# Decode attention with an MLP on one Trainium2 core: which queue issues wq, x, b2 and the first K tiles, and what the second K tile waits for

## The chip, the cores and the metric

The kernel runs on 1 core of one Trainium2 chip. The metric is the device time of one execution in microseconds. Beside the times there is one profiled execution. Its span is counted from the first to the last instruction of the program, and all positions in time below are counted from the start of that span.

## The reference

One decode step for 8 sequences (B = 8, one query each): layernorm, attention over a cache of 4096 keys with 32 heads of 128, an MLP on the same normalized input, and a residual. All inputs are bf16.

```python
def _A_ref(x, k_cache, v_cache, wq, wo):          # caches: 8 x 32 x 4096 x 128
    q = (x @ wq) as 8 x 32 x 1 x 128
    scores = jnp.einsum("bhqd,bhkd->bhqk", q, k) * (Dh ** -0.5)
    p = _softmax(scores, axis=-1)
    o = jnp.einsum("bhqk,bhkd->bhqd", p, v)
    return o as 8 x 1 x 4096 @ wo

def _B_ref(x, w1, b1, w2, b2):                     # w1: 640 x 1728, w2: 1728 x 640
    y = _layernorm(x, axis=-1)
    h = _gelu(jnp.einsum("bsd,df->bsf", y, w1) + b1)
    return jnp.einsum("bsf,fd->bsd", h, w2) + b2

xn = _layernorm(x, axis=-1)                        # x: 8 x 1 x 640
return x + _A_ref(xn, ...) + _B_ref(xn, ...)
```

Each cache has 268 MB, wq and wo 5.24 MB each, w1 and w2 2.2 MB each. Every byte of them is needed once.

## The kernel before

The work is cut into 32 tiles (`NQ`), one for each pair of a sequence and a group of 8 heads. A tile needs 8.39 MB of K and 8.39 MB of V, each as 128 partitions of 64 KB. SBUF holds three slots of that size: `KA` and `KB` for K tiles of even and odd number, and `VS` for V. In what follows K0, K1, V0 and so on are the tiles by number.

The slots hold other things before their first tile. `wq_sb` lies in `VS` (line 269), so V0 may only be loaded once the q matmuls have read it. `b2_sb`, `x_sb`, the two normalized inputs, the masks' scratch and a block of zeros lie in `KB` (lines 280 to 290), so K1 may only be loaded once these have been read. K0 goes to `KA`, which is free from the start.

For a tile, VectorE multiplies 176 of the 256 key positions of each partition with q, adds halves and sums (`dve_chunk`, three chunks), while TensorE, ScalarE and TensorE again transpose, copy and multiply the other 80 (`pe_T`, `act_T`, `pe_QK`). `dve_max` forms the maximum, `act_exp` the exponentials with their sums, `pe_PV` multiplies with V in 256 matmuls, `act_O` and `o_norm` finish the tile's output.

The program is written as steps with a position each (`at(pos, step)`, lines 791 to 882). The steps are sorted by position, and each engine's list of instructions is what the steps give it in that order. An engine runs its list in order and stops at a wait. VectorE, ScalarE and TensorE have their tiles' part as a hardware loop; SyncE and GpSimd have theirs written out. A wait that an engine has already made for the same or a later count of the same semaphore is left out (`_Eng.wait`, line 51).

SyncE's list before: wq (position -890), K0 (-870), a wait for the q matmuls (`tk["qmm"]`, set in `pe_q`), K1 (position 49), V0 (50; its own wait for `qmm` is left out, being made already), then for each further tile K(i) (position 100i - 51) and V(i) (100i + 50). `load_k` for i from 2 on waits for the last transposes and the last VectorE chunk of tile i - 2 (`kt`, `km`); `load_v` for i from 1 on waits for the PV matmuls of tile i - 1 (`pv`). The order is K0, K1, V0, K2, V1, K3, V2 and so on, each behind the one before it in the one queue. Behind the caches follow w1, w2 and wo: w1 and w2 wait for tile 30's K slot, wo for tile 31's.

ScalarE's list before begins with the loads of x (-900) and b2 (-898). Then it loads a table and takes the square roots for the two layernorms (`norm`).

TensorE's list at the start: `pe_xT(0)` transposes the normalized x, `pe_xT(1)` the twice normalized one for the MLP, `pe_acc0` sets the accumulator `ACC_ps` to x + b2 by 11 matmuls that read zeros, `x_sb` and `b2_sb`, and `pe_q` computes q by 160 matmuls once wq has landed. `cp_q` (VectorE) copies q to SBUF, `qrep` (GpSimd) spreads tile 0's part of it, `pe_qbc` and `act_qbc` bring that to all partitions, and `dve_chunk(0, 0)` needs both this and K0.

In the tail, `pe_mlp1` computes the hidden layer into `HT_ps` (14 blocks of 8 columns; the last is the remainder of 1728 after 13 blocks of 128), `act_gelu` applies gelu in one instruction for 13 blocks and one for the last, and `pe_mlp2` adds its product with w2 to `ACC_ps`. The rows of wo are added in `fin_wl` and `fin_wn`, and `fin_store` writes the result.

Of the kernel before, what the change touches and what calls it, by code (L numbers as in the profile page):

```python
# [11 lines left out]
ACT = mybir.ActivationFunctionType  # L12
AX = mybir.AxisListType

P = 128
# [177 lines left out]
def bass_parallel_sum__gqa_block_cached__mixer_channel_mlp__decode_kernel(  # L193
# [13 lines left out]
    B, _, D = A_x.shape  # L207
# [8 lines left out]
    DC = D // P  # L216
    FB = F // P
# [23 lines left out]
    def kslot(i):  # L241
        return KA if i % 2 == 0 else KB
# [5 lines left out]
    x2 = A_x.rearrange("b s d -> (b s) d")  # L248
    out2 = out.rearrange("b s (c n) -> (b s c) n", n=P)

    with ExitStack() as es:
# [7 lines left out]
        def part(slot, lo, n, rows=P):  # L259
            return S_sb[0:rows, slot, lo:lo + n]  # L260
# [3 lines left out]
        def scratch(n, rows=P, slot=KB):  # L264
            ap = part(slot, o_[slot], n, rows)
            o_[slot] += n + n % 2
            return ap

        wq_sb = part(VS, 0, DC * H * DH).rearrange("p (c n) -> p c n", c=DC)
        w1_sb = scratch(DC * F, P, KA).rearrange("p (c n) -> p c n", c=DC)  # L270
        w2_sb = scratch(FB * D, P, KA).rearrange("p (c n) -> p c n", n=D)
        hT_sb = scratch((FB + 1) * B, P, KA).rearrange("p (c b) -> p c b", b=B)
# [7 lines left out]
        b2_sb = scratch(D, 1)  # L280
        x_sb = scratch(D, B)
# [11 lines left out]
        ones_sb = sb("ones_sb", [1, B], BF)  # L293
# [35 lines left out]
        ACC_ps = ps("ACC_ps", [P, 512], F32)  # L329
# [3 lines left out]
        HT_ps = TR_ps[:, 1, :].bitcast(F32)[:, 0:(FB + 1) * B]  # L333
# [4 lines left out]
        pe, dve, act, sp, pool = (_Eng(sem(f"{n}_s")) for n in ("pe", "dve", "act", "sp", "pool"))  # L338
        pe2, act2 = _Eng(sem("pe2_s")), _Eng(sem("act2_s"))
        ld_s = [_Dma(sem(f"ld_s{s}")) for s in range(3)]  # L340
        ld_x, ld_b1, ld_b2, ld_wq, ld_w1, ld_w2a, ld_w2b, st_o = (
            _Dma(sem(n)) for n in ("ld_x", "ld_b1", "ld_b2", "ld_wq", "ld_w1", "ld_w2a", "ld_w2b", "st_o"))
# [3 lines left out]
        tk = {}  # L346
        prog = []

        def at(pos, fn, *a):
            prog.append((pos, len(prog), fn, a))  # L350
# [4 lines left out]
        def cache_src(cache, i):  # L355
            hq, b = divmod(i, B)
            return cache[b, hq * HS:(hq + 1) * HS].rearrange("h (p j) d -> (h p) j d", j=NKEY)

        def load_k(i):
            s = kslot(i)  # L360
            if i >= 2:
                sp.wait(tk[("kt", i - 2)], tk[("km", i - 2)])
            elif s == KB:
                sp.wait(tk["qmm"])
            tk[("k", i)] = ld_s[s].sig(sp.dma_start(tile[s], cache_src(A_k_cache, i)))

        def load_mlp():
# [123 lines left out]
        def pe_acc0():  # L491
            pe.wait(tk["consts"], tk["x"], tk["b2"], tk["id"])
            pe.matmul(ACC_ps[:, 0:DC * B], zeros_sb, zeros_sb[:, 0:DC * B], start=True, stop=False,
                      skip_group_check=True)
            for c in range(DC):
                pe.matmul(ACC_ps[:, c * B:(c + 1) * B], x_sb[:, c * P:(c + 1) * P], ident_bf[0:B, 0:B],
                          start=False, stop=False, skip_group_check=True)
                pe.matmul(ACC_ps[:, c * B:(c + 1) * B], b2_sb[:, c * P:(c + 1) * P], ones_sb[:, :],
                          start=False, stop=False, skip_group_check=True)

        def widen():
            pool.wait(tk["w1"], tk["b1"])
# [19 lines left out]

        def act_gelu():
            TRB[1].use(act)
            act.activation(hT_sb[:, 0:FB, :].rearrange("p c b -> p (c b)"), HT_ps[:, 0:FB * B],
                           ACT.Gelu_apprx_tanh)
            tk["h"] = TRB[1].used(act, act.sig(act.activation(
                hT_sb[:, FB, :], HT_ps[:, FB * B:(FB + 1) * B], ACT.Gelu_apprx_tanh)))

# [259 lines left out]


        Q = 100.0
        at(-900, load, "x", ld_x, x_sb, x2, act)
        at(-898, load, "b2", ld_b2, b2_sb, B_b2.rearrange("(o f) -> o f", o=1), act)
        at(-890, load, "wq", ld_wq, wq_sb, A_wq.rearrange("(p c) n -> p c n", c=DC))
        at(NQ * Q - 55, load_mlp)
        at(-870, load_k, 0)
        at(-798, zero_w2b)
        at(-800, consts_pool)
# [7 lines left out]
        at(-773, pe_xT, 1)  # L806
        at(-772, cp_xT, 1)
        at(-771, pe_acc0)
        at(-770, pe_q)
        at(-765, cp_q)  # L810
        at(NQ * Q - 11.8, load_b1)
        at(NQ * Q - 11.7, widen)
        at(NQ * Q - 11.5, pe_mlp1)
        at(NQ * Q - 11, act_gelu)
        at(NQ * Q + 4.6, pe_mlp2, range(FB))
        for i in range(NQ):
            o = i * Q
            last = i == NQ - 1
            if i:
                at(o - 51, load_k, i)  # L820
            at(o + 50, load_v, i)
            at(o - 52, qrep, i)
            at(o - 2, k_ready, i)
            at(o - 11, pe_qbc, i)
            at(o - 10.5, act_qbc, i)
            nt = jp_of(i) // TPB
            w = 42.0 / nt
            for t in range(nt):
                at(o + w * t, pe_T, i, t)
                at(o + w * (t + 0.4), act_T, i, t)  # L830
                at(o + w * (t + 1.5), pe_QK, i, t)
            at(o + 2, dve_chunk, i, 0)
            at(o + 26, dve_chunk, i, 1)
            at(o + 52, dve_sel, i, 0)
            at(o + 55, dve_sel, i, 1)
            at(o + 58, dve_chunk, i, 2)
            at(o + 84, dve_max, i)
            at(o + 90 if i else o + Q + 45, act_exp, i)
            at(o + Q + 48, pe_RS, i)
            at(o + Q + 57, dve_rinv, i)  # L840
            at(o + Q + 50, pe_PV, i)
            if not last:
                at(o + Q + 71, act_O, i)
            at(o + Q + 75, o_norm, i)
# [3 lines left out]
        o = NQ * Q  # L848
# [78 lines left out]
```

## Time and profile before

| | us |
|---|---|
| median of 3 runs (lowest, highest) | 1282.06 (1282.04, 1282.07) |
| the profiled execution's own time | 1281.86 |
| its span | 1280.5 |
| VectorE busy | 1104.0 |
| TensorE busy | 672.4 |
| ScalarE busy | 476.3 |
| GpSimd busy | 105.0 |

Nearly every row of the profile names line 111, because a helper replays all recorded instructions from there; the groups are told apart by the tiles that they write and read. `S_sb` is the tensor with the three slots, `KT_sb` and `TR_ps` belong to the transposes, `S_ps` to the scores of TensorE's share, `PV_ps` to the product with V, `CH_ps` to q, `ACC_ps` to the final sums. `SPq` and `ACTq` rows are DMA issues by SyncE and ScalarE. In a row of the timeline the first number is the start, the second the length, both in us, then the engine, the instruction, output and inputs and their shapes; in brackets stands how long the engine had been idle and what ended it. One row can merge several instructions (x2, x160), and then its length runs from the start of the first to the end of the last. The trace also holds a record of each packet that a DMA engine moved, with its start, length, bytes and queue; q1 is SyncE's queue, q10 ScalarE's.

### The profile page before, as it was taken

The page shows a single profiled execution, that of the slowest core. Times are in us where ns is not written, and L with a number is a line of the kernel's source. Part 1 is how long each engine was busy: PE and PEld are TensorE (multiplying, and loading weights), DVE is VectorE, ACT ScalarE, POOL GpSimd, SP SyncE. Part 2 cuts the span into 40 slices and gives each one's busy share as a digit, 9 for nine tenths or more (in the row PEclk, how much of TensorE's full clock was granted, in tenths as well). Part 3 has the DMA queues.
Part 4 walks back from the last instruction along what each step waited for, and adds up shares of the span by engine and source line. Part 5 has one row for each costly group of instructions (what it writes and reads, how often), then busy time and mean ns, then how long its engine had stood idle before and what let it go on. Part 6 is the DMA issues. An engine that isn't in the chain of part 4 may idle for free.

```text
span 1280.5 us, 34441 instructions
## 1 busy us (share of the span) xinstructions
PE 672.4 (53%) x13944; PEld 576.2 (45%) x13944; DVE 1104.0 (86%) x680; ACT 476.3 (37%) x905; POOL 105.0 (8%) x113
## 2 busy tenths in 40 slices
PE   1546555446645446545456555456454466454476
PEld 1435444335535345434345444345344355353365
DVE  1899999889888889888899888898888898888895
ACT  0524444233444233443234443234443234442331
POOL 0020000000000000000000000000000000000040
PEclk9755555555555555555556555555655565555555
DMA  9999999999999999999999999999999999999998
GB/s 423 423 435 428 434 432 434 436 432 432 430 442 432 432 430 442 428 434 432 440 428 432 434 434 436 430 434 430 442 430 430 432 442 430 432 430 444 423 436 364
DMA packets 10675, 551.99 MB, mean 431 GB/s; under 512 B 1244, under 2 KB 1445, under 8 KB 1702
## 3 DMA queue, kind: packets, MB, share of 16 engines
q1 hardware_dynamic: 10592, 551.79, 99.7%
q8 instruction: 9, 0.15, 0.0%
q10 hardware_dynamic: 70, 0.03, 0.0%
q14 instruction: 4, 0.03, 0.0%
HBM read 551.80 MB, written 0.01 MB: 431 GB/s over the span
## 4 chain that ended last, share of the span: by engine, by line
DMA 52%; DVE 36%; issue 11%; DVEq 0%; PE 0%; SPq 0%; ACT 0%
DMA S_sb<-in_A_k_cache_dram 51%; DVE S_sb L111 26%; DVE Sd_sb L111 8%; DMA S_sb<-in_A_wo_dram 2%; DVE S_ps L111 1%; DVE ri_sb L111 0%; DVEq L109 0%; PE ACC_ps L111 0%; DVE mx_sb L111 0%; SPq L111 0%; DVE mbT_sb L111 0%; DVE mxT_sb L111 0%; DVE mq_sb L111 0%; DVE mb_sb L111 0%; PE QB_ps L111 0%
## 5 line engine op out<-in xcount | busy, mean ns | idle before, releaser
L111 PE MATMUL TR_ps<-ident_bf,S_sb 128*128 128x128 bf16 (+1 forms) x2570 | 343.3, 285 | 354.0 <-POOL kr_sb L111 342.7
L111 DVE TENSOR_TENSOR S_sb<-S_sb,qbc_sb 128x7552 bf16<-128x7552 bf16 (+1 forms) x96 | 392.5, 4088 | 128.5 <-DMA S_sb<-in_A_k_cache_dram 128.1
L111 PEld LDWEIGHTS TR_ps<-ident_bf,S_sb 128*128 (+2 forms) x2570 | 245.7, 104 | 411.3 <-issue 338.6
L111 DVE TENSOR_REDUCE Sd_sb<-S_sb 128x59 f32<-128x3776 bf16 (+1 forms) x96 | 390.2, 4065 | 6.0
L111 ACT ACTIVATE KT_sb<-TR_ps 128x1024 bf16<-128x1024 bf16 x320 | 326.7, 1023 | 122.3 <-PE TR_ps L111 110.4
L111 PE MATMUL PV_ps<-P_sb,S_sb 128*128 128x8 bf16 x8192 | 224.0, 175 | 135.6 <-DMA S_sb<-in_A_v_cache_dram 133.1
L111 PEld LDWEIGHTS PV_ps<-P_sb,S_sb 128*128 128x128 bf16 x8192 | 221.4, 103 | 138.3 <-DMA S_sb<-in_A_v_cache_dram 135.7
L111 DVE TENSOR_TENSOR S_sb<-S_sb 128x3776 bf16<-128x3776 bf16 (+1 forms) x96 | 205.4, 2139 | 3.3
L111 ACT ACTIVATE P_sb<-Sd_sb,NB_sb 128x256 bf16<-128x256 f32 x256 | 126.3, 494 | 214.6 <-DVE NB_sb L111 214.6
L111 PE MATMUL S_ps<-qrep_sb,KT_sb 128*128 128x8 bf16 x2560 | 122.3, 177 | 52.1 <-ACT KT_sb L111 49.0
L111 ACT ACTIVATE oU_sb<-PV_ps 128x8 f32<-128x8 f32 x31 | 5.5, 177 | 375.0 <-PE PV_ps L111 375.0
L111 PEld LDWEIGHTS S_ps<-qrep_sb,KT_sb 128*128 128x128 bf16 x2560 | 92.4, 104 | 83.7 <-ACT KT_sb L111 40.5
L111 POOL TENSOR_TENSOR oT_sb<-oU_sb,ri_sb 128x8 bf16<-128x8 f32 x31 | 71.7, 2312 | 374.8 <-DVE S_sb L111 315.3
L111 POOL COPY qrep_sb<-qT_sb 128x128 bf16<-128x128 bf16 x32 | 18.1, 566 | 474.2 <-PE S_ps L111 455.5
L111 ACT ACTIVATION_READ_ACCUMULATOR P_sb<-Sd_sb,NB_sb 128x1 f32 x256 | 47.8, 187 | 0.0
L111 DVE TENSOR_TENSOR S_ps<-S_ps,mask_sb 128x320 f32<-128x320 f32 (+1 forms) x65 | 31.6, 486 | 2.6 <-PE S_ps L111 2.6
L111 DVE TENSOR_REDUCE Sd_sb<-S_ps 128x40 f32<-128x320 f32 x64 | 31.5, 492 | 2.2
L111 PE MATMUL QB_ps<-ident_bf,qrep_sb 128*128 128x128 bf16 x32 | 9.1, 284 | 40.6 <-DVE S_sb L111 21.4
L111 ACT ACTIVATE qbc_sb<-QB_ps 128x128 bf16<-128x128 f32 x32 | 8.9, 277 | 57.1 <-PE QB_ps L111 57.1
L111 POOL MEMSET kr_sb<- 128x1 f32 x32 | 3.1, 98 | 295.0 <-DMA S_sb<-in_A_k_cache_dram 295.0
L111 PEld LDWEIGHTS QB_ps<-ident_bf,qrep_sb 128*128 128x128 bf16 x32 | 3.3, 103 | 43.4 <-ACT oU_sb L111 26.5
L111 PE MATMUL CH_ps<-rs_sb,ones_f 128*128 128x8 f32 x64 | 16.8, 337 | 6.4 <-ACT P_sb L111 6.4
(73 smaller groups left out, 149.0 us busy)
## 6 DMA issues: line engine op xcount, KB each, us to landing
S_sb<-in_A_v_cache_dram SPq DMA_DIRECT2D x1, 6144.0 KB, 26.8
S_sb<-in_A_wq_dram SPq DMA_DIRECT2D x1, 5120.0 KB, 15.3
S_sb<-in_A_wo_dram SPq DMA_DIRECT2D x1, 2560.0 KB, 15.8
S_sb<-in_B_w_dram SPq DMA_DIRECT2D x1, 2160.0 KB, 30.3
S_sb<-in_B_w_dram SPq DMA_DIRECT2D x1, 2080.0 KB, 34.8
S_sb<-in_A_v_cache_dram SPq DMA_DIRECT2D x1, 2048.0 KB, 31.3
S_sb<-in_A_wo_dram SPq DMA_DIRECT2D x1, 1280.0 KB, 18.5
S_sb<-in_A_wo_dram SPq DMA_DIRECT2D x1, 800.0 KB, 20.0
```

What stands on the lines that cost most here:

```text
L111: inst = getattr(e, name)(*a, **k)
```

## The change

The first loads change queues: x and b2 go from ScalarE's list to SyncE's, wq from SyncE's to ScalarE's. The positions stay, so that SyncE's list begins with x, b2, K0 and ScalarE's with wq.

`pe_acc0` gets a signal on its last matmul (`tk["acc0"]`), and K1 waits for that instead of the q matmuls. V0's own wait for the q matmuls now stands in SyncE's list, between K1 and V0.

`act_gelu` takes the 13 blocks in two instructions (6 and 7 blocks), so that gelu has three.

```diff
@@ load_k
             elif s == KB:
-                sp.wait(tk["qmm"])
+                sp.wait(tk["acc0"])
             tk[("k", i)] = ld_s[s].sig(sp.dma_start(tile[s], cache_src(A_k_cache, i)))
@@ pe_acc0
             for c in range(DC):
                 pe.matmul(ACC_ps[:, c * B:(c + 1) * B], x_sb[:, c * P:(c + 1) * P], ident_bf[0:B, 0:B],
                           start=False, stop=False, skip_group_check=True)
-                pe.matmul(ACC_ps[:, c * B:(c + 1) * B], b2_sb[:, c * P:(c + 1) * P], ones_sb[:, :],
-                          start=False, stop=False, skip_group_check=True)
+                last = pe.matmul(ACC_ps[:, c * B:(c + 1) * B], b2_sb[:, c * P:(c + 1) * P], ones_sb[:, :],
+                                 start=False, stop=False, skip_group_check=True)
+            tk["acc0"] = pe.sig(last)
@@ act_gelu
-            act.activation(hT_sb[:, 0:FB, :].rearrange("p c b -> p (c b)"), HT_ps[:, 0:FB * B],
-                           ACT.Gelu_apprx_tanh)
+            for lo, hi in ((0, FB // 2), (FB // 2, FB)):
+                act.activation(hT_sb[:, lo:hi, :].rearrange("p c b -> p (c b)"), HT_ps[:, lo * B:hi * B],
+                               ACT.Gelu_apprx_tanh)
@@ the steps
-        at(-900, load, "x", ld_x, x_sb, x2, act)
-        at(-898, load, "b2", ld_b2, b2_sb, B_b2.rearrange("(o f) -> o f", o=1), act)
-        at(-890, load, "wq", ld_wq, wq_sb, A_wq.rearrange("(p c) n -> p c n", c=DC))
+        at(-900, load, "x", ld_x, x_sb, x2)
+        at(-898, load, "b2", ld_b2, b2_sb, B_b2.rearrange("(o f) -> o f", o=1))
+        at(-890, load, "wq", ld_wq, wq_sb, A_wq.rearrange("(p c) n -> p c n", c=DC), act)
```

## The prediction

> **What bounds the kernel now.** I read the page's head first, for the span and the share of the DMA engines, then its list of queues, then the timeline of the first 140 us, and last the timeline of the tail.
>
> ```profile
> span 1280.5 us, 34441 instructions
> ...
> PE 672.4 (53%) x13944; PEld 576.2 (45%) x13944; DVE 1104.0 (86%) x680; ACT 476.3 (37%) x905; POOL 105.0 (8%) x113
> ...
> DMA  9999999999999999999999999999999999999998
> ...
> q1 hardware_dynamic: 10592, 551.79, 99.7%
> ...
> HBM read 551.80 MB, written 0.01 MB: 431 GB/s over the span
> ```
>
> VectorE is busy for 86% of the span, but the 16 DMA engines are busy in every slice, and SyncE's queue alone fills 99.7% of them. The windows view gives 433 GB/s for each of 300:600, 600:900 and 8:1270. So the time is a start of about 2 us, 552 MB at 433 GB/s, and a short tail. A change of issue order can move that only if it starts the stream earlier or later, lets the queue run empty, or lengthens the tail.
>
> ```profile
> 0.74 0.38 SPq L111 DMA_DIRECT2D S_sb<-in_A_wq_dram  x1
> 0.75 0.59 ACTq L111 DMA_DIRECT2D S_sb<-in_A_x_dram  x1
> ...
> 1.18 19.71 SPq L111 DMA_DIRECT2D S_sb<-in_A_k_cache_dram  x2
> ...
> 16.10 4.43 PE L111 MATMUL CH_ps<-xT_sb,S_sb 128*128 128x8 bf16 x160 [7.76 <-DMA S_sb<-in_A_wq_dram]
> 20.57 0.42 DVE L111 CAST qT_sb<-CH_ps 128x256 bf16<-128x256 f32 x1 [12.51 <-PE CH_ps L111]
> 20.93 0.44 SPq L111 DMA_DIRECT2D S_sb<-in_A_v_cache_dram  x1
> ...
> 21.73 0.28 ACT L111 ACTIVATE qbc_sb<-QB_ps 128x128 bf16<-128x128 f32 x1 [14.96 <-PE QB_ps L111]
> 35.78 4.03 DVE L111 TENSOR_TENSOR S_sb<-S_sb,qbc_sb 128x7424 bf16<-128x7424 bf16 x1 [14.79 <-DMA S_sb<-in_A_k_cache_dram]
> ```
>
> The columns are start, length, engine, what ran, and in brackets the wait. wq lands at 16.1, q's chain ends at 22.0, and VectorE then idles until K0 lands at 35.78: 13.8 us of slack between wq and the first VectorE work. K1 was issued at about 20.5 (the end of the 19.71 us row that covers K0 and K1) and landed at 55.5, so for 15 us it stood behind K0 in a full queue.
>
> ```profile
> 68.57 0.33 SPq L111 DMA_DIRECT2D S_sb<-in_A_k_cache_dram  x1
> 84.51 0.33 SPq L111 DMA_DIRECT2D S_sb<-in_A_v_cache_dram  x1
> 102.80 0.33 SPq L111 DMA_DIRECT2D S_sb<-in_A_k_cache_dram  x1
> 128.13 0.33 SPq L111 DMA_DIRECT2D S_sb<-in_A_v_cache_dram  x1
> ```
>
> These are SyncE's issues of K2, V1, K3 and V2. The tile view's landing times put V0 at 74.8 (20.93+53.9), K2 at 94.2 (68.57+25.6), V1 at 113.5 (84.51+29.0), K3 at 132.8 (102.80+30.0). Each new issue is in time while the transfer ahead of it is unfinished. The margins are 6.2 us for K2, 9.7 for V1, 10.7 for K3 and 4.7 for V2; later ones grow, V3 is issued at 162.56 with K4 landing near 172. All four issues descend from VectorE's first start: K2 and K3 wait for its last chunk of K0 and K1, V1 and V2 for the PV of a head group whose exponentials wait for its maximum.
>
> **The change part by part.** The sum is made against the profiled execution, 1281.86 us (span 1280.5 and 1.36 around it); the median of the three times is 0.20 more, 1282.06.
>
> Start of the stream: wq is issued first on ScalarE's queue (0.75) instead of SyncE's (0.74). ScalarE's first issue took 0.59, SyncE's 0.38; the trace's packet records have x, from ScalarE, starting 0.94 us after its issue and wq 1.02. Bounds -0.2 to +0.2; I take 0, as the two rows agree.
>
> x and b2 on SyncE: they hold it for 0.59 and 0.23 by ScalarE's rows, so K0 goes out at about 1.6 instead of 1.18. wq's packets cover that; without them it would cost 0.4. x may wait for one wq packet (1.51), putting the sums of x and b2, done now at 8.3, near 10. Nothing waits for them but K1.
>
> K1 at about 10 instead of 20.5: 0. K0 and wq hold the engines until 35.8 in either order, and the bytes ahead of K1 are the same. Behind K1 on SyncE stands V0, which still waits for the q matmuls; wherever these end before about 53, K1's transfer covers V0's issue.
>
> wq beside K0: this is the part that costs. Before, both stood in one queue and wq had the engines to itself. Now two queues share each engine. In the packet records one engine's share of a cache tile is 8 rows of 64 KB at 2.42 us, of wq 8 rows of 40 KB at 1.51. How two queues alternate shows once: b2's packet, from the other queue, ran at 5.58 between two wq rows, and its 4-byte semaphore packet at 7.15, one wq row later, with no loss between. So they alternate row by row, the semaphore takes a turn of its own, and one row already fetched goes first. wq's semaphore then comes behind seven of K0's eight rows, 2.4 us before the slowest engine's last row (35.0 to 35.3): wq lands at 32.6 to 32.9. With 0.4 to the first matmul and the 5.95 us of q's chain (16.10 to 22.05), VectorE starts at 39.1, which is 3.3 us late. Bounds: two queues sharing by bytes would land wq near 26 (2x5.24 MB at 433 GB/s, from 1.8), and VectorE would lose nothing; strict turns put wq's semaphore behind K0's last row, and VectorE starts at 41.5, 5.7 late. I take 3.3, the order that b2's record shows.
>
> The Trainium skill, page "DMA: Bandwidth & Descriptors", section "Queues, rings and completion order", says that an engine takes turns between queue rows by whole packets of typically 9 to 17 descriptors. By that, wq's eight rows and semaphore would go through in one turn, VectorE would not be late, and the sum would be 0; b2's packet between two wq rows at 5.58 speaks against it.
>
> Where the 3.3 us go: K2 is issued at 71.9 and V2 at 131.4, both still before the landings of V0 (74.8) and K3 (132.8). But a landing is the slowest engine's. In the records most engines finish V0 at 72.5 and the three slowest at 74.0 to 74.3; K3's end for the slowest is 132.4. An empty queue takes 1.0 us from issue to first packet, up to 2.3 for the last engine (wq's first packets start from 1.76 to 3.06), and the first packet ran 0.54 longer (2.06 against 1.51). So the slowest engine may pass from V0 to K2 at 74.7 instead of 74.3 (71.9+2.3+0.54), and from K3 to V2 between 132.4 (131.4+1.0, no loss) and 134.3 (131.4+2.3+0.54, 1.9 lost in all). I take +0.6, nearer the lower end, since nine of wq's sixteen first packets started within 1.2 us of the issue and fast engines can idle without moving the end. VectorE itself catches up: it works 34.5 us a tile against 38.7 between landings.
>
> Gelu: three instructions instead of two, about 0.2 us more (the pair took 0.33, a small one 0.18).
>
> ```profile
> 1250.82 0.33 ACT L111 ACTIVATE S_sb<-TR_ps 128x104 bf16<-128x104 f32 x2 [10.93 <-PE TR_ps L111]
> 1251.17 1.28 ACT L111 ACT_TABLE_LOAD   x1
> 1257.37 0.51 ACT L111 ACTIVATE P_sb<-Sd_sb,NB_sb 128x256 bf16<-128x256 f32 x1 [4.92 <-DVE NB_sb L111]
> ...
> 1276.65 0.83 PE L111 MATMUL ACC_ps<-oS_sb,S_sb 128*128 128x8 bf16 x25 [0.36 <-DMA S_sb<-in_A_wo_dram]
> ```
>
> ScalarE's 4.92 us of idle time hide it, and TensorE takes up gelu's output at 1252.4 after other work. Without that cover it would cost 0.2. The end waits for wo, the last bytes of the stream.
>
> Sum: 0 + 0 + 0 + 0.6 + 0 = +0.6, so 1282.5 for a profiled run and **1282.7** beside the median.
>
> **Rivals.** *wq lands late enough to empty the queue (slower).* With strict turns VectorE starts at 41.5. K2 goes out at 74.3 and V2 at 133.8; V2's first packets come from 134.8 to 136.7 (1.0 to 2.3+0.54 later) where the slowest engine was free at 132.4. That is 2.4 to 4.3 us, say +3.3: 1285.4. For it: the semaphore's own turn at 7.15. Against it: b2's record has one fetched row going first. It decides from a VectorE start about 3.3 us late on, and passes 0.2% at 4 to 5.8 us late.
>
> *The move is hidden wholly (no change).* If the queues share by bytes, or wq runs in one turn, q is ready before K0 lands and no issue moves: 1282.1. For it: 13.8 us of slack now. Against it: b2 between two rows.
>
> *The stream gets tighter (faster).* Two queues could fill the engines that now start late (1.76 to 3.06 us) and even out the spread at V0's end (72.5 to 74.3). At best 1.3 us at the head and about as much in the lag, together 2.6; I give it -1.0: 1281.1. Against it: the slowest engine needs the same bytes.
>
> That the earlier K1 does nothing is part of the forecast.
>
> **How the numbers follow.** Forecast 0.50, slower rival 0.24, hidden 0.18, faster 0.08. The range reaches from 1281.4, part of the way into the faster case, to 1285.8, past the middle of the slower one; the forecast's own range is 1282.0 to 1284.1. 0.2% is 2.56 us, about what a measurement of this kernel can tell from no change. Beyond it lie 0.04 of the faster case, and of the slower ones 0.19 of the rival and 0.02 of the forecast: faster 0.04, same 0.75, slower 0.21.
>
> **What would show it.** wq's first matmul near 33 rather than 16 shows the shared queue; VectorE's first product at 39 shows what it costs. K1's landing should stay at 55.5 although its issue moves to about 10. K2's issue near 72 and V2's near 131.4, and the landings of K2 (94.2) and K3 (132.8) up to 2 us later, show or refute the emptied queue. The last K tile's landing (now 1216.6) must move by the same amount as the end, and TensorE must still wait for wo at the last sums. A first product of VectorE past 40, a slice of the DMA line that is not full, or a stream at another rate than 433 GB/s would make the prediction wrong.

## The result and the profile after

| | before | after |
|---|---|---|
| median, us | 1282.00 | 1284.87 |
| lowest to highest | 1281.79 to 1282.07 | 1284.16 to 1285.77 |
| runs | 13 | 13 |
| span of the profiled execution | 1280.5 | 1283.5 |

The changed kernel is slower by 2.87 us: the ratio is 1.0023, with a 95% interval from 1.0015 to 1.0030, which lies around the 0.2% that the prediction drew as its line. The spread is news too. The kernel before stays within 0.3 us from run to run, the changed one moves over 1.6.

The page of the changed kernel, head and queues:

```profile
span 1283.5 us, 34442 instructions
...
DMA  9999999999999999999999999999999999999998
...
q1 hardware_dynamic: 10466, 546.55, 98.6%
q10 hardware_dynamic: 196, 5.26, 1.0%
q8 instruction: 9, 0.15, 0.0%
...
HBM read 551.80 MB, written 0.01 MB: 430 GB/s over the span
```

The bytes are the same, the DMA line is digit for digit that of before, and the mean rate fell from 431 to 430 GB/s. A loss of 3 us in 1283 is too small for a line of tenths; it has to be looked for where an issue comes late. The timeline of SyncE's issues after:

```profile
0.74 0.40 SPq L111 DMA_DIRECT2D S_sb<-in_A_x_dram  x1
1.20 0.23 SPq L111 DMA_DIRECT2D S_sb<-in_B_b_dram  x1
1.48 7.40 SPq L111 DMA_DIRECT2D S_sb<-in_A_k_cache_dram  x2
37.47 0.33 SPq L111 DMA_DIRECT2D S_sb<-in_A_v_cache_dram  x1
71.81 0.33 SPq L111 DMA_DIRECT2D S_sb<-in_A_k_cache_dram  x1
87.74 0.33 SPq L111 DMA_DIRECT2D S_sb<-in_A_v_cache_dram  x1
106.03 0.33 SPq L111 DMA_DIRECT2D S_sb<-in_A_k_cache_dram  x1
131.05 0.33 SPq L111 DMA_DIRECT2D S_sb<-in_A_v_cache_dram  x1
```

K1 is out at 8.5 (its issue takes the last 0.35 us of the row that covers K0 and K1), V0 at 37.5; K2 moved from 68.57 to 71.81, V2 from 128.13 to 131.05. The same timeline around VectorE's first work:

```profile
33.01 4.43 PE L111 MATMUL CH_ps<-xT_sb,S_sb 128*128 128x8 bf16 x160 [24.51 <-DMA S_sb<-in_A_wq_dram]
...
37.48 0.42 DVE L111 CAST qT_sb<-CH_ps 128x256 bf16<-128x256 f32 x1 [29.51 <-PE CH_ps L111]
...
38.64 0.28 ACT L111 ACTIVATE qbc_sb<-QB_ps 128x128 bf16<-128x128 f32 x1 [31.95 <-PE QB_ps L111]
39.02 4.02 DVE L111 TENSOR_TENSOR S_sb<-S_sb,qbc_sb 128x7424 bf16<-128x7424 bf16 x1 [1.12 <-ACT qbc_sb L111]
```

VectorE's first product now waits for q, no longer for K0, and starts at 39.02 instead of 35.78. Where the time goes is seen in the landings of later K tiles, by GpSimd's markers (`k_ready`), before and then after:

```profile
171.60 0.10 POOL L111 MEMSET kr_sb<- 128x1 f32 x1 [6.21 <-DMA S_sb<-in_A_k_cache_dram]
210.30 0.10 POOL L111 MEMSET kr_sb<- 128x1 f32 x1 [10.20 <-DMA S_sb<-in_A_k_cache_dram]
```

```profile
174.41 0.10 POOL L111 MEMSET kr_sb<- 128x1 f32 x1 [5.80 <-DMA S_sb<-in_A_k_cache_dram]
213.29 0.10 POOL L111 MEMSET kr_sb<- 128x1 f32 x1 [9.97 <-DMA S_sb<-in_A_k_cache_dram]
```

K4 lands 2.8 us later, K5 3.0; K31, the last, landed at 1219.66 against 1216.65, again 3.0. So nearly all is lost before 174 us and nothing is won back. The windows view around the passage from V0 to K2 and from K3 to V2, before and then after (the last two columns are the busy share of the DMA engines and GB/s):

```profile
72.00:80.00 8.00, 5.38 (x179) 5.31 (x180) 7.93 (x3) 2.21 (x10) 2.21 (x1) 0.50 1.02 438
131.00:139.00 8.00, 2.32 (x16) 1.66 (x16) 7.76 (x9) 0.08 (x1) 0.14 (x2) 0.50 0.97 418
```

```profile
72.00:80.00 8.00, 2.63 (x84) 2.54 (x82) 7.76 (x9) 4.04 (x16) 0.29 (x1) 0.50 0.97 389
131.00:139.00 8.00, 2.63 (x18) 1.77 (x17) 7.93 (x3) 0.46 (x2) 2.97 (x2) 0.50 0.98 377
```

The view counts a packet whole in the window in which it begins. With each packet's time and bytes divided at the window's edges, the first window goes from 429 to 395 GB/s at a share of 1.00 and then 0.98, the second from 431 to 362 at 1.00 and then 0.95: both lose far more of their rate than of their busy share. The packet records say why a busy engine moves less: in the changed kernel K2's first rows begin between 72.9 and 74.7, and 14 of the 16 run longer than the usual 2.42 us, 3.0 at the median. V2's first rows begin between 132.0 and 134.6 (130.6 to 132.4 before), 15 of 16 run long, 3.1 at the median, and here most second rows take 2.6 to 2.9 too. An engine that is handed its next row late idles a little (by the order of ends and starts up to about 0.7 us at K2 and 1.3 at V2; the records do not name the engine) and then runs a row slowly, and the profile counts the slow row as busy. By the slowest engine, V1's end is 1.1 us late and V2's first row 2.2.

### The profile page after: what moved, and what is told of

Same layout as the page of the kernel before. It is cut to its first block, busy times and chain, and to the rows that moved or that the text cites. A ratio compares the mean times of both kernels' runs of the same rounds, so it can differ in the third digit from the quotient of the medians.

```text
span 1283.5 us, 34442 instructions
## 1 busy us (share of the span) xinstructions
PE 671.6 (52%) x13944; PEld 574.3 (45%) x13944; DVE 1103.9 (86%) x680; ACT 476.3 (37%) x906; POOL 101.2 (8%) x113
## 4 chain that ended last, share of the span: by engine, by line
DMA 52%; DVE 36%; issue 11%; PE 1%; DVEq 0%; SPq 0%; ACT 0%; POOL 0%
DMA S_sb<-in_A_k_cache_dram 48%; DVE S_sb L111 26%; DVE Sd_sb L111 7%; DMA S_sb<-in_A_wq_dram 3%; DMA S_sb<-in_A_wo_dram 2%; DVE S_ps L111 1%; PE CH_ps L111 0%; DVE ri_sb L111 0%; DVEq L109 0%; PE ACC_ps L111 0%; DVE mx_sb L111 0%; SPq L111 0%; DVE mxT_sb L111 0%; DVE mbT_sb L111 0%; PE QB_ps L111 0%
## 5 line engine op out<-in xcount | busy, mean ns | idle before, releaser
L111 POOL COPY qrep_sb<-qT_sb 128x128 bf16<-128x128 bf16 x32 | 16.1, 502 | 494.6 <-PE S_ps L111 459.0
```

Of the source, the lines that this page charges most:

```text
L111: inst = getattr(e, name)(*a, **k)
```

## The experiments

Theory A is the prediction's chain: wq shares the engines with K0, q is late, VectorE starts 3.3 us late, and the queue runs short ahead of K2 and V2. Theory B: two queues cost by themselves. Theory C: the earlier K1 or gelu costs.

**The three loads back on their queues** (`e1_one_queue`), the rest of the change kept:

```diff
-        at(-900, load, "x", ld_x, x_sb, x2)
+        at(-900, load, "x", ld_x, x_sb, x2, act)
         (b2 likewise)
-        at(-890, load, "wq", ld_wq, wq_sb, A_wq..., act)
+        at(-890, load, "wq", ld_wq, wq_sb, A_wq...)
```

> The changed kernel with the three first loads back on their old queues (wq on SyncE's, x and b2 on ScalarE's); the earlier K1 and gelu in three instructions stay. Theory A (wq shares the engines with K0, lands at 33, VectorE starts 3.3 us late, and the queue runs empty ahead of K2 and V2): wq lands at 16, VectorE starts at 35.8, K2 is issued at 68.6, V2 at 128.1, and the time is 1282.0 (within 0.3). Theory B (two queues cost by themselves in the first 35 us, whatever VectorE does): 1282.0 too. Theory C (the earlier K1 or gelu costs, in the head or the tail): 1283 to 1284.9.

Measured: 1282.03 us, ratio 1.0000 (0.9991 to 1.0010). wq's first matmul is at 16.03, K2 goes out at 68.68, V2 at 128.18. The earlier K1 and the third gelu instruction together cost and bring nothing; theory C is out.

**The queues alone** (`e2_queues_only`): the kernel before, with the three loads moved and nothing else, so that K1 still waits for the q matmuls.

```diff
-        at(-900, load, "x", ld_x, x_sb, x2, act)
+        at(-900, load, "x", ld_x, x_sb, x2)
         (b2 likewise)
-        at(-890, load, "wq", ld_wq, wq_sb, A_wq...)
+        at(-890, load, "wq", ld_wq, wq_sb, A_wq..., act)
```

> The kernel before with the queues of the first loads changed and nothing else; K1 still waits for the q matmuls. Theory A: q's matmuls end at 37.4, so K1 is issued at 37.5, 2 to 4 us after the engines have finished K0 (33.8 to 35.3). The queue runs empty there instead of ahead of K2 and V2: with 1.0 from issue to first packet, 0.7 for a slower first packet and up to 0.3 for the second, 4 to 5 us are lost at once, K1 lands near 59.5, K2 (issued at 71.8) and V2 (131.1) are then early enough, and the time is 1286 to 1287. Theory B: as the changed kernel, 1284.9, plus whatever the late K1 costs. Theory C: the queues alone cost nothing, 1282.0.

Measured: 1287.43 us, ratio 1.0042 (1.0025 to 1.0059), 5.5 us slower than before, 2.6 slower than the changed kernel and somewhat above the 1286 to 1287 that theory A gave. SyncE's timeline, and the windows view of 34 to 39 us:

```profile
1.48 36.50 SPq L111 DMA_DIRECT2D S_sb<-in_A_k_cache_dram  x2
38.02 0.43 SPq L111 DMA_DIRECT2D S_sb<-in_A_v_cache_dram  x1
71.96 0.33 SPq L111 DMA_DIRECT2D S_sb<-in_A_k_cache_dram  x1
```

```profile
34.00:39.00 5.00, 4.13 (x141) 4.04 (x139) 0.42 (x1) 0.21 (x1) 0.33 (x2) 1.00 0.53 174
```

K1 goes out at 37.6. In the packet records K0's last row ends at 35.2 and K1's first begins at 38.6, with no cache row between; the 174 GB/s of the view are rows that begin in the window's last 0.4 us. This is the whole loss, in one place: K1's shift of 5.4 us (it lands at 60.8 instead of 55.5) makes K2 and V2 early enough again. So the new wait of K1 is what the new queues need: alone it is worth nothing, with them it saves 2.6 us of 5.5.

**K0 behind the sums of x and b2** (`e3_k0_behind_acc0`): the changed kernel, with K0 issued at 8.3, so that wq has a start of several rows.

```diff
-            elif s == KB:
+            else:
                 sp.wait(tk["acc0"])
...
-        at(-870, load_k, 0)
+        at(-760, load_k, 0)
```

> The changed kernel with K0 issued behind the wait for the sums of x and b2, at about 8.4 instead of 1.5; wq stays on ScalarE's queue and still shares the engines with K0, but with five of its eight rows ahead. Theory A: wq lands at 20 to 25, q is ready before K0 lands (about 35.5), VectorE starts at 35.8 as before, K2 goes out at 68.6 and V2 at 128.1, no packet runs slow there, and the time is 1282.0 to 1282.4. Theory B: the two queues still run beside each other, for a third of the rows; 1283 to 1284.9. Theory C: 1284.9.

Measured: 1281.97 us, ratio 1.0000 (0.9990 to 1.0009). The timelines of TensorE and VectorE and of SyncE:

```profile
22.58 4.43 PE L111 MATMUL CH_ps<-xT_sb,S_sb 128*128 128x8 bf16 x160 [14.30 <-DMA S_sb<-in_A_wq_dram]
```

```profile
35.85 4.03 DVE L111 TENSOR_TENSOR S_sb<-S_sb,qbc_sb 128x7424 bf16<-128x7424 bf16 x1 [8.38 <-DMA S_sb<-in_A_k_cache_dram]
```

```profile
68.64 0.33 SPq L111 DMA_DIRECT2D S_sb<-in_A_k_cache_dram  x1
```

The two queues still share the engines, and wq lands 6.5 us later than before. VectorE again waits for K0, not for q, and nothing is lost. The two queues cost nothing here, where q beats K0; theory B is out.

**VectorE late with all loads as before** (`e4_dve_late3`): three products of 128x2048 ahead of the first chunk.

```diff
+        def dve_busy(n):
+            dve.wait(tk["fill"], tk[("k", 0)])
+            for _ in range(n):
+                t = dve2.sig(dve.tensor_tensor(P_sb[:, :, :], P_sb[:, :, :], P_sb[:, :, :], ALU.mult))
+                dve.wait(t)
...
+        at(1.9, dve_busy, 3)
```

> The kernel before, all loads and queues as they were, with three added VectorE products of 128x2048 (about 1.1 us each by the rate of the 128x7552 one, together 3.3) between K0's landing and its first chunk. wq lands at 16 and no load is moved. Theory A: K2 is issued near 71.9 and V2 near 131.4, packets there run 2.8 to 3.5 us instead of 2.42, and the time is 1284.5 to 1285.5, as the changed kernel. Theory B: VectorE catches up within three tiles, 1282.0. Theory C: 1282.0.

Measured: 1285.92 us, ratio 1.0030 (1.0019 to 1.0041). VectorE's timeline and SyncE's:

```profile
36.00 3.74 DVE L111 TENSOR_TENSOR P_sb<-P_sb 128x2048 bf16<-128x2048 bf16 x3 [15.06 <-DMA S_sb<-in_A_k_cache_dram]
39.78 4.02 DVE L111 TENSOR_TENSOR S_sb<-S_sb,qbc_sb 128x7424 bf16<-128x7424 bf16 x1
```

```profile
72.57 0.33 SPq L111 DMA_DIRECT2D S_sb<-in_A_k_cache_dram  x1
...
132.06 0.33 SPq L111 DMA_DIRECT2D S_sb<-in_A_v_cache_dram  x1
```

The products took 3.74 us and VectorE's first chunk began at 39.78, 4.0 late instead of 3.3. K2 went out at 72.57, V2 at 132.06; all 16 of K2's first rows ran long (3.1 at the median) and 14 of V2's. A late VectorE makes the loss with no load moved. The size, 3.96 us for 4.0, is above what was expected.

**One and five products** (`e5_dve_late1`, `e6_dve_late5`), for the point from which it costs:

> The kernel before with one added VectorE product ahead of its first chunk instead of three; by the run with three (K2 out 4.0 us late, at 72.57) VectorE is 1.3 late. Theory A (only an emptied queue costs): K2 goes out at 69.9, its first packet would be ready at 70.9, before the engines finish V0 (72.5); V2 goes out at 129.4, ready at 130.4, as the fastest engines finish K3 (130.6). Nothing runs dry and the time is 1282.0 (within 0.3). Rival (the time follows VectorE's start, us for us): 1283.3.

> The same with five products, VectorE 6.6 us late: K2 out at 75.2, V2 at 134.7. Theory A: past the margin each further us of VectorE costs one. Against the run with three products, 3.96 slower at 4.0 late, 2.6 more: 6.6 slower, 1288.5 (1287.8 to 1289.2). If the loss were one fixed price for restarting the queue, it would stay at 1286.

Measured: 1283.06 us with one product, 1.1 slower (ratio 1.0009, 1.0000 to 1.0019), and 1288.31 with five, 6.35 slower (1.0047, 1.0031 to 1.0064). The second fits theory A. The first is a miss: nothing should have run short at 1.3 us late, and the rival, us for us, came nearer. SyncE's timeline with one product:

```profile
69.89 0.33 SPq L111 DMA_DIRECT2D S_sb<-in_A_k_cache_dram  x1
...
129.12 0.33 SPq L111 DMA_DIRECT2D S_sb<-in_A_v_cache_dram  x1
```

K2 goes out 2.6 us before the first engines finish V0 (72.5), and still 14 of its 16 first rows run long, 2.6 at the median; 7 of V2's do. So theory A has to be mended: an issue needs more lead than the 1.0 us to its first packet.

**Late only after K2** (`e7_late_after_k2`): the three products behind tile 0's last chunk.

```diff
+            dve.wait(tk["fill"], tk[("km", 0)])
...
+        at(83, dve_busy, 3)
```

> The kernel before with the three products placed behind the last chunk of tile 0, so that K2 goes out at 68.6 as before and only V1, K3 and V2 come from a VectorE that is 4.0 us late. The queue can run dry only ahead of V2 (out near 132.1). If V2's place sets the loss: 1285.5 to 1286, as with the products ahead of tile 0. If both places add up, with about 1 us from K2: 1284.5 to 1285. If K2's place sets it: 1282.0.

Measured: 1284.04 us, ratio 1.0017 (1.0008 to 1.0027), 2.1 slower. K2 went out at 68.62 and 15 of its first rows ran at 2.42; V2 went out at 131.75 and all 16 ran long. This lies in none of the three bands, but of the three readings it is nearest to the middle one: V2's place alone costs 2.1 at 3.6 us late. That K2's place costs the rest of the 4.0 is a difference of two runs; the packet records of `e4_dve_late3` agree with it, where the slowest engine ends V1 1.8 us late and V2 3.6 late.

**Only K2 late, VectorE on time** (`e8_k2_after_nb`, `e9_k2_after_exp`): SyncE waits longer ahead of K2, and nothing else is touched.

```diff
-                sp.wait(tk[("kt", i - 2)], tk[("km", i - 2)])
+                sp.wait(tk[("kt", i - 2)], tk[("km", i - 2)], tk[("nb", 0)] if i == 2 else None)
```

with `exp` in place of `nb` in the second.

> The kernel before with one more wait on SyncE: K2 also waits for the bias of tile 0's exponentials, so that it goes out at about 70.2 instead of 68.6, while VectorE, V1, K3 and V2 stay where they were. Theory A1 (an issue must be about 4 us ahead of the end of the transfer before it, or the packets there run slow, although the queue is not yet empty): with 2.3 us of lead to 72.5, first packets of 2.5 to 3.3 us ahead of K2, time 1282.4 to 1283.1. Theory A0 (1.0 us of lead is enough, as the prediction had it): 1282.0.

> The same with a wait for tile 0's exponentials: K2 goes out at about 74.3, 1.8 us after most engines have finished V0 and 5.7 later than before; V2 stays where it was. Theory A1: loss 74.3 + 1.0 to the first packet + 0.7 + 0.3 for two slow packets, against a slowest engine that was free at 74.3, up to 1 more for stragglers: 2 to 3, and the shift gives V2 more lead, so nothing is added there: 1284 to 1285. A loss of us for us with the issue would give 1287.7, a loss from VectorE's lateness alone 1282.0.

Measured: 1282.78 us for the first, 0.75 slower (ratio 1.0005, 0.9996 to 1.0015; its ten runs reach from 1282.40 to 1283.53, the 18 of before from 1281.90 to 1282.43), and 1285.46 for the second, 3.4 slower (1.0026, 1.0016 to 1.0036), somewhat above the expected band. In both, VectorE's first product starts as before (35.83 and 35.78). SyncE's issue of K2 in the first and in the second, and the window behind it in the first:

```profile
70.27 0.33 SPq L111 DMA_DIRECT2D S_sb<-in_A_k_cache_dram  x1
```

```profile
74.31 0.33 SPq L111 DMA_DIRECT2D S_sb<-in_A_k_cache_dram  x1
```

```profile
72.00:80.00 8.00, 5.35 (x179) 5.29 (x180) 7.93 (x3) 2.26 (x10) 2.25 (x1) 0.50 0.96 395
```

With VectorE on time and K2 out 2.2 us ahead of V0's end, the view gives 395 GB/s instead of 438 (408 instead of 429 with packets divided at the edges), in an execution that was the slowest of the ten. The first run's interval still includes no change; the second, 3.4 us slower with VectorE on time, shows that the issue's lead counts, and not VectorE as such. The kernels together, without `e2_queues_only`, whose V0 ends 5.4 us later; K2's part is from the packet records of one execution each, the change of time from the medians:

```
kernel             K2 out  lead to 72.5  long first rows  their median  V2 out  time
before              68.57       3.9          0 of 16          2.42      128.13    0
e3_k0_behind_acc0   68.64       3.9          1                2.42      128.15   +0.0
e1_one_queue        68.68       3.8          1                2.42      128.18   +0.1
e7_late_after_k2    68.62       3.9          1                2.42      131.75   +2.1
e5_dve_late1        69.89       2.6         14                2.61      129.12   +1.1
e8_k2_after_nb      70.27       2.2         15                2.69      128.18   +0.8
after               71.81       0.7         14                3.00      131.05   +2.9
e4_dve_late3        72.57      -0.1         16                3.07      132.06   +4.0
e9_k2_after_exp     74.31      -1.8         13                3.17      128.14   +3.4
e6_dve_late5        74.98      -2.5         16                3.08      134.54   +6.4
```

A row counts as long above 2.45 us. Between a lead of 3.8 us and one of 2.6 K2's first rows stop running at full pace. The lead works engine by engine. Over the first rows of K2, V1, K3 and V2 in all eleven kernels, ends and starts matched in order of time: with less than 1 us between the issue and the engine's own end 90 of 93 ran long, 3.1 at the median; from 1 to 2 us 27 of 31, 2.9; from 2 to 3 us 38 of 54, 2.6; from 3 to 4 us 6 of 53; above that 10 of 473. The kernel before stands at this edge already. Its K2 is in time, but at V2 the first engine ends K3 2.5 us after the issue, and three of the first rows run 2.5 to 3.0 us, on engines that are early and do not set the end.

## Why the prediction was right, and where it was too small

The path was right in each of its steps up to the late issues. wq's landing was put at 32.6 to 32.9 and its first matmul followed at 33.01; VectorE was put at 39.1 and started at 39.02; K2 was put at 71.9 and V2 at 131.4, and they went out at 71.81 and 131.05. The order of the rows was read from one packet of b2 between two rows of wq, and it held: after two rows of wq the records have K0's and wq's rows in turn, and wq's last semaphore packet at 32.6, behind seven of K0's rows. An estimate by the Trainium skill's rule of whole packets of typically 9 to 17 descriptors (page "DMA: Bandwidth & Descriptors", section "Queues, rings and completion order"), which would let wq's rows through in one turn, puts wq's landing near 16; this trace disagrees, with the first q matmul at 33.01.

The start of the stream cost nothing, as said, and so did the earlier K1 and gelu: the gelu instructions took 0.39 us instead of 0.33 and ScalarE's wait behind them is still 4.89. The 0 for the earlier K1 was right with the queues of before (`e1_one_queue`). With the new queues it is what saves 2.6 us (`e2_queues_only`); the prediction's reason, that the bytes ahead of K1 are the same, does not say so, because the price arises only where K1 waits for a late q.

The term that was mis-sized is the emptied queue. The prediction put K2's passage at +0.4, took +0.6 in all and gave 1.9 as the most. Measured were 2.9: by the slowest engine 1.1 us at V1's end, the rest, 1.8, at V2. The step that was too small is the passage itself: "an empty queue takes 1.0 us from issue to first packet, up to 2.3 for the last engine", with a first packet 0.54 longer. The 1.0 is right (V2, out at 131.05, has its first rows from 132.01). But the last engine's first row began 2.9 us after the issue at K2 and 3.5 at V2, and first rows ran about 0.6 us longer at the median, up to 1.0. And an issue 1.0 us ahead is not yet in time: with less than about 3 us of lead most first rows run 2.6 to 3.2 us at the median instead of 2.42. This shows in `e5_dve_late1` and `e8_k2_after_nb` too, where the queue was hardly empty. That most second rows run slowly too (2.6 to 2.9) shows at V2 of the changed kernel alone; in `e2_queues_only`, `e4_dve_late3`, `e7_late_after_k2` and `e9_k2_after_exp` the queue ran empty and the second rows took 2.42 at the median. The reason for taking the lower end, that fast engines can idle without moving the end, did not hold either: the last rows to begin were slow ones. With that, the margins of 6.2 and 4.7 us, read from landings, were no margins: a VectorE 1.3 us late costs 1.1, 3.2 late 2.9, 4.0 late 4.0, 6.4 late 6.4.

The range, 1281.4 to 1285.8, held the time, but only because it had been stretched towards the slower rival: 1284.87 lies above the forecast's own range of 1282.0 to 1284.1, and nearer to the rival's 1285.4 than to 1282.7. That the range held is in part luck. Most of the chance, 0.75, was on a change within 0.2%, and the median came out at 0.22%, with an interval on both sides of that line. The slower rival had the right place (K2 and V2 from an emptied queue) and the wrong cause for its size: wq did not land with K0's last row, VectorE was not 5.7 us late, and 3.2 were enough, where the prediction had 0.2% passed only from 4 us on.

Left open is what in the path from an issue to its rows needs the lead of about 3 us, and why three engines of the 16 end V2 1.4 to 2.0 us behind the median in the changed kernel. No run looks into the time between an issue and its first row.

## What to carry to other kernels

When a kernel's one full queue is the bound, read each issue's lead over the end of the transfer ahead of it, by the single engines' ends and not by the landing; here rows ran slowly with less than about 3 us of lead even where the queue hardly ran empty. A transfer that moves to a second queue may no longer go first: here wq took turns with K0, row by row, its matmuls began at 33.0 instead of 16.1, and whatever waits for it moved with that. An early wait that looks free in one order can be what another order needs, so try the parts of a change apart and together.

## What the runs showed that was not expected

A DMA engine's row can run slow without any other queue's packets: at V2 of the changed kernel the records from 131 to 137 us are of q1 alone, and the first 64 KB rows take 3.1 us at the median instead of 2.42, counted as busy. The busy share of the DMA engines hardly falls while the rate does (1.00 to 0.98 against 429 to 395 GB/s at K2), so the rate shows it better than the share.

Some of the slow engines that set a landing are slow for another reason. The page's queue q8, of kind instruction, moves 16 KB at a time. In the kernel before eight such packets begin before 102 us. Each takes 0.96 to 0.99 us of one engine, and the row behind it 2.9 to 3.0 instead of 2.42. The engines of those at 60.58 and 70.28 end V0 at 74.1 and 74.2, where eleven end by 72.9. So the spread between engines that the prediction read at V0's end comes at least in part from these.

Once a few microseconds are lost ahead of tile 4, none returns in 27 tiles, although VectorE has 4 us to spare in each: K4 lands 2.8 us late, and K31 3.0.

The kernels that issue late at K2 or V2 are also those whose time scatters: 1.6 us from run to run in the changed kernel and 0.9 to 2.1 in `e4_dve_late3` to `e9_k2_after_exp`, against 0.3 to 0.5 for the kernel before and for the one with K0 behind the sums. `e2_queues_only`, which loses its time at K1, stays within 0.3 in its four runs.
